# Attention's first step put in another order on all engines, and the weight sums of blocks 0 and 1 of the first expert started elsewhere

## The chip, the cores and the metric

The kernel runs on one core of one Trainium2 chip. The metric is the time of one execution in device microseconds (us). The core has five engines with a queue of their own each, which they work off in order: TensorE (PE, matrix products and transposes), VectorE (DVE), ScalarE (ACT), GpSimd (POOL) and SyncE (SP, which here only starts DMAs). They wait for each other through semaphores.

## The reference

Everything is fp32. Two batches, eight heads, 576 rows of 64 numbers; 128 random features. The result of the attention goes through a mixture of four experts and then through a layer with a cosine.

```
def phi(x):
    h = x @ omega.T - sum(x * x) / 2          # x scaled by 64 ** -0.25
    return exp(h - max(h)) / sqrt(128)
kv  = phi(k).T @ v ;  z = sum(phi(k))         # per batch and head
x   = (phi(q) @ kv) / (phi(q) @ z + 1e-6)     # 1152 tokens x 512

for e in 0..3:
    out += p[:, e] * (relu(x @ w1[e]) @ w2[e])    # p: domain_probs, normalised
h = out @ w_in ;  result = (h * cos(h)) @ w_out   # w_in, w_out given in float64
```

## The kernel before, in words

Products of full precision are made from three products of a rounded part (`...h`) and a rest (`...l`): hi x hi, hi x lo, lo x hi. ACT makes the rounded part with a copy, DVE or POOL the rest with a subtraction. So `xTh`/`xTl` are the parts of a transposed block of keys or queries, `sth`/`stl` those of a hidden activation `h`, `w1h`/`w1l` those of a weight.

Attention runs over eight pairs of heads (index `s`, a batch and two heads, 512 rows each) and one last block, the tail: the 64 rows of each batch that are left, of all heads (`kL`, `qL`). The loop over `s` (0 to 10) is a pipeline written out by hand: in step `s` it makes the key features of pair `s` (`features`: projection `pj_k` on PE, maximum `mx` and bias `nb` on DVE, exponentials `phk` on ACT), then the query features of pair `s` (`phq`), transposes pair `s+1` (`turn`), multiplies keys and values of pair `s-1` (`kv_of`), and so on. The squared norms come from POOL (`norms`, `x_k` and `x_q`) and end in a small sum on DVE (`sq`). Step 0 also makes the features of the tail's keys (`phiL`); step 1 multiplies them with the values (`kv_tail`: `kvL`).

The first expert's products are a stream of quanta (some six products each) that starts in step 6: each step calls it four times (`dense_quanta`), and after attention it runs alone. What has to be loaded or prepared is bound to a quantum's number by `start_at(e, q, ...)` in `plan`; `advance` moves each such job on by one yield per quantum. `load_a(0, p, "s")` starts a load of block `p` of `w1` at its quantum, and five quanta later makes four sums of its quarters (`rs`, the "weight sums"), which expert 0 needs for a scheme with fewer products for two thirds of its tokens (from quantum 28 on). For expert 0 sums and rest are on POOL. The loads take their buffers from a ring of three (`rawp`), and so does the job that makes the sums.

[...] The queue of each engine follows the order in which the code issues its instructions; there is no other scheduler.

The tail's transposes at the end of attention are `tx_L`; the divided result they take is `xsL`, its products are `numL`, and `pTL` are the transposed query features of the tail. `T1` to `T4` are sums of token blocks, made by DVE behind attention (`token_sums`).

Of the kernel before, what the change touches and what calls it, by code (L numbers as in the profile page):

```python
# [26 lines left out]
def performer_moe_kernel(ctx, tc, q, k, v, omega, probs, w1, w2, w_in, w_out, out):  # L27
# [4 lines left out]
    E, _, F = w1.shape  # L32
# [27 lines left out]
    late = {}  # L60

    def bank(name):
        return ps.tile([P, 512], F32, tag="ps", name=name)
# [51 lines left out]
    def split(eng, src, hi, lo):  # L115

        nc.scalar.activation(hi, src, ACTF.Copy)  # L117
        yield
        eng.tensor_tensor(out=lo, in0=src, in1=hi.bitcast(F32), op=ALU.subtract)  # L119
# [555 lines left out]
    def quantum_at(columns):  # L675
        return next(q for q in range(FROM64, sum(QE)) if columns_to(q) - columns_to(FROM64) >= columns)

    def start_at(e, q, make, *args):
        while q >= QE[e]:
            q -= QE[e]  # L680
            e += 1
        starts[e].setdefault(q, []).append(lambda: make(*args))

    def plan():
        start_at(0, 13, load_a, 0, 0, "s")
        start_at(0, 20, load_a, 0, 1, "s")
        start_at(0, 27, load_a, 0, 2)
        start_at(0, 35, load_a, 0, 3)
        for e in range(1, E + 2):
            for p, q in enumerate((51, 61) if e == 1 else (50, 60)):  # L690
                start_at(e - 1, q, load_a, e, p)
            for u, q in enumerate((0, 9, 23, 26)):
                start_at(e, q, load_v2 if e < E else load_v64, e, u)
            start_at(e, 6, load_a, e, 2)
            start_at(e, 17, load_a, e, 3)
        halves = [
            (kind, e, u, z)
            for e in (E, E + 1) for kind in "av" for u in range(NU) for z in range(2)
        ]
        at = 0  # L700
        for kind, e, u, z in halves:
            q = quantum_at(at)
            lead = quantum_at(at + LOAD64) - q
            at += A_GAP if kind == "a" else V_GAP
            start_at(0, q, lambda k=(kind, e, u), z=z, l=lead: convert64(k, z, l))
        start_at(E - 1, 58, second_x, 1)
        start_at(E - 1, 69, second_sums)
        start_at(E, 3, second_x, 0)

    plan()  # L710

    under = []
# [37 lines left out]
    with tc.tile_pool(name="at1", bufs=1) as at1, tc.tile_pool(name="at2", bufs=2) as at2:  # L750
# [5 lines left out]
        def warm(n):  # L756
            for _ in range(n):
                nc.tensor.matmul(wps[:, :P], zero, zero, start=True, stop=True)
# [64 lines left out]
        def norms(nm, t):  # L823

            x2 = at2.tile([P, 2 * R, D], F32, tag=f"x2{nm[0]}", bufs=1, name=f"x2_{nm}")
            nc.gpsimd.tensor_tensor(out=x2, in0=t, in1=t, op=ALU.mult)
            sq = at2.tile([P, 2 * R], F32, tag="sq", name=f"sq_{nm}")
            w = D
            while w > 8:
                w //= 2  # L830
                nc.gpsimd.tensor_tensor(
                    out=x2[:, :, 0:w], in0=x2[:, :, 0:w], in1=x2[:, :, w : 2 * w], op=ALU.add
                )
            yield
            nc.vector.tensor_reduce(out=sq, in_=x2[:, :, 0:w], op=ALU.add, axis=AX.X)
            yield sq

        def turn(nm, t):

            tp = bank(f"tp_{nm}")  # L840
            for i in range(R):
                nc.tensor.transpose(tp[:, i * P : (i + 1) * P], t[:, 2 * i : 2 * i + 2, :], ident)

            def split(xh=None, xl=None):
                if xh is None:
                    xh = at2.tile([P, R * P], F32R, tag="xTh", name=f"xTh_{nm}")
                    xl = at2.tile([P, R * P], F32R, tag="xTl", name=f"xTl_{nm}")
                nc.scalar.activation(xh, tp, ACTF.Copy)
                nc.vector.tensor_tensor(out=xl, in0=tp, in1=xh.bitcast(F32), op=ALU.subtract)
                return xh, xl  # L850

            return split
# [69 lines left out]
        NPR = len(pairs)  # L922
        xss, phks, phqs, kts, qts = {}, {}, {}, {}, {}
# [129 lines left out]
        def norms_ahead(nm, t):  # L1053
            sqs[nm] = norms(nm, t)
            next(sqs[nm])
# [5 lines left out]
        fk = fq = iter(())  # L1061
        turned = {}

        def turn_ahead(s):
            splits = []
            if s == 0:
                omega_pairs()
            if s < NPR and ("k", s) not in turned:
                splits.append(("k", turn(f"k{s}", kts[s])))
            if s == 0:  # L1070
                warm(1)
            splits.append(("q", turn(f"q{s}", qL if s == NPR else qts[s])))
            if s == 0:
                warm(1)
            for x, split in splits:
                if s == 0 and x == "q":
                    late["q0"] = split
                else:
                    turned[x, s] = split()

        def query_features(s):
            phqs[s] = at1.tile([P, 2 * R, M], F32, tag="phq", name=f"phq_{s}")
            steps = features(f"q{s}", turned.pop(("q", s)), phqs[s])
            next(steps)
            return steps
# [4 lines left out]
        for s in range(NPR + 3):  # L1090
            for _ in fq:
                pass
            if s < first:
                advance(wload)
            dense_quanta(s, DQ)
            kvs = kv_of(s - 1) if 1 <= s <= NPR else iter(())
            next(kvs, None)
            if s != 1:
                next(kvs, None)
            if s >= first:  # L1100
                advance(wload)
            dense_quanta(s, DQ)
            fk = iter(())
            if s < NPR:
                phks[s] = at1.tile([P, 2 * R, M], F32, tag="phk", name=f"phk_{s}")
                fk = features(f"k{s}", turned.pop(("k", s)), phks[s])
                next(fk)
            if s == 0:

                turned["kL"] = turn("kL", kL)(xkL[:, 0, :], xkL[:, 1, :])  # L1110
                turned["q", 0] = late.pop("q0")()
                norms_ahead("kL", kL)
                phiL = at1.tile([P, H, M], F32, name="phiL")
                fL = features("kL", turned.pop("kL"), phiL)
                next(fL)
            if s == 1:
                kv_tail(phiL)
                next(kvs, None)
            if s + 1 < NPR:
                norms_ahead(f"k{s + 1}", kts[s + 1])  # L1120
            if s < NPR:
                norms_ahead(f"q{s + 1}", qL if s + 1 == NPR else qts[s + 1])
            dense_quanta(s, DQ)
            next(fk, None)
            if 1 <= s <= NPR:
                turn_phi(s - 1)
            elif s == NPR + 1:
                tail_turn_phi()
            next(fk, None)
            px = iter(())  # L1130
            if 2 <= s <= NPR + 1:
                b, hp = pairs[s - 2]
                px = put_x(f"{s - 2}", hp, xss.pop(s - 2), b * R, R)
            elif s == NPR + 2:
                px = tail_put_x()
            next(px, None)
            fq = iter(())
            if s == 0:
                turned["k", 1] = turn("k1", kts[1])()
            if s <= NPR:  # L1140
                fq = query_features(s)
            for _ in px:
                pass
            dense_quanta(s, DQ)
            if s < NPR:
                turn_ahead(s + 1)
            if s == 0:
                for _ in fL:
                    pass
            if 1 <= s <= NPR:  # L1150
                nums(s - 1)
            elif s == NPR + 1:
                tail_nums()
            if s + 2 < NPR:
                load(s + 2)
            if s + 1 < NPR:
                load_v(s + 1)
            advance(wload)
            if s < 2 * NU:
                wload.append(load_a(0, s, "p") if s < NU else load_v2(0, s % NU))  # L1160
                advance(wload)
            if s == 1:
                nc.vector.tensor_reduce(out=psum_, in_=pr, op=ALU.add, axis=AX.X)
                nc.vector.tensor_scalar(out=psum_, in0=psum_, scalar1=1e-9, scalar2=None, op0=ALU.add)
                nc.vector.reciprocal(out=psum_, in_=psum_)
                nc.vector.tensor_tensor(
                    out=pn, in0=pr, in1=psum_.to_broadcast([P, NTILE, E]), op=ALU.mult
                )
# [38 lines left out]
```

## Time and profile before

| | |
|---|---|
| time, median of 3 runs | 671.59 us (670.2 to 671.76) |
| the profiled execution | 671.61 us, its span 669.8 us |
| PE busy | 660.6 us, 99% of the span |
| DVE busy | 526.2 us, 79% |
| ACT busy | 322.1 us, 48% |
| POOL busy | 183.8 us, 27% |

Attention fills the first 110 us or so of the span; with step 6, at about 60 us, the expert's products come in between. In a row of the timeline stand the start and the duration, the engine, the line, the operation, what it writes and reads, and how often it follows itself; in brackets how long the engine had idled before it, and for whom. Products are pipelined: a product's duration is longer than the distance to the next.

### The profile page before, as it was taken

What the parts mean: (1) busy time and instruction counts of PE and PEld (TensorE: products, weight loads), DVE (VectorE), ACT (ScalarE), POOL (GpSimd) and SP (SyncE); (2) the same over time, 40 slices, a digit from 0 to 9 for tenths busy, and PEclk for the clock granted to TensorE, in tenths of its full rate; (3) what the DMA queues carried; (4) which work ended last, traced back from release to release, by engine and by line L of the source; (5) the groups of instructions that cost most, each with busy time, mean ns of one, the idle gap of its engine ahead of it and who ended that gap; (6) DMA issues with size and microseconds to landing.
All of it is one profiled execution on the core that took longest, in us unless ns stands there. A gap on an engine that the chain in (4) does not pass through costs nothing.

```text
span 669.8 us, 9978 instructions
## 1 busy us (share of the span) xinstructions
PE 660.6 (99%) x3639; PEld 604.9 (90%) x3639; DVE 526.2 (79%) x965; ACT 322.1 (48%) x634; POOL 183.8 (27%) x231
## 2 busy tenths in 40 slices
PE   8999999899999999999999999999999999999998
PEld 8899998798899988899988999888999888999887
DVE  5998648879979879889899788788677793496962
ACT  5777664435433544345343354444365663355530
POOL 8778443401220111111111111100044340144420
PEclk9999999899999999999999999999999999999999
DMA  8654201231534533435525336310711000700111
GB/s 191 190 143 110 81 12 34 78 99 63 189 128 156 188 106 115 172 125 173 160 95 171 117 129 213 110 48 1 312 34 32 0 1 20 295 1 1 47 48 47
DMA packets 55441, 70.95 MB, mean 106 GB/s; under 512 B 15200, under 2 KB 40032, under 8 KB 55392
## 3 DMA queue, kind: packets, MB, share of 16 engines
q1 hardware_dynamic: 46800, 40.92, 19.8%
q0 software_dynamic: 8448, 29.37, 13.0%
q8 instruction: 28, 0.46, 0.3%
q14 instruction: 21, 0.17, 0.1%
q10 hardware_dynamic: 144, 0.03, 0.0%
HBM read 55.36 MB, written 14.94 MB: 105 GB/s over the span
## 4 chain that ended last, share of the span: by engine, by line
PE 87%; DVE 7%; POOL 2%; ACT 2%; issue 1%; DMA 0%; DVEq 0%; POOLq 0%
PE g L583 42%; PE g L431 13%; PE num L973 2%; PE g_0a L431 2%; PE g_0c L431 2%; PE g_1a L431 2%; PE kv L944 2%; PE g_3a L431 2%; PE g_1c L431 2%; PE g_3c L431 2%; PE g_2a L431 2%; PE g_2c L431 2%; PE pj_q L867 1%; PE pj_k L867 1%; PE g_0e L431 1%
## 5 line engine op out<-in xcount | busy, mean ns | idle before, releaser
L381 POOL TENSOR_TENSOR rtf64r<-rtf64r 128x384 f32<-128x384 f32 x32 | 38.4, 1199 | 117.5 <-DVE rtf64r L378 73.6
L555 ACT ACTIVATE sth<-h 128x512 fp32r<-128x512 f32 x72 | 44.8, 627 | 50.5 <-PE g L583 46.1
L556 DVE SCALAR_TENSOR_TENSOR stl<-h,sth 128x512 fp32r<-128x512 f32 x72 | 51.8, 724 | 11.3 <-ACT sth L555 9.6
L119 DVE TENSOR_TENSOR stl<-h,sth 128x512 fp32r<-128x512 f32 x36 | 35.3, 985 | 13.7 <-ACT sth L117 13.7
L583 PE MATMUL g<-v2h,stl 128*128 128x512 f32 (+1 forms) x110 | 42.9, 390 | 2.6 <-DVE stl L556 2.3
L583 PE MATMUL g<-v3h,sth 128*128 128x512 f32 (+1 forms) x110 | 43.1, 392 | 0.0
L583 PE MATMUL g<-v3l,sth 128*128 128x512 f32 (+1 forms) x110 | 42.9, 390 | 0.0
L583 PE MATMUL g<-v0h,stl 128*128 128x512 f32 (+1 forms) x110 | 42.7, 388 | 0.1
L583 PE MATMUL g<-v3h,stl 128*128 128x512 f32 (+1 forms) x110 | 42.7, 388 | 0.0
L583 PE MATMUL g<-v2h,sth 128*128 128x512 f32 (+1 forms) x110 | 42.7, 388 | 0.0
L583 PE MATMUL g<-v2l,sth 128*128 128x512 f32 (+1 forms) x110 | 42.6, 388 | 0.0
L583 PE MATMUL g<-v0h,sth 128*128 128x512 f32 (+1 forms) x110 | 42.6, 387 | 0.0
L583 PE MATMUL g<-v0l,sth 128*128 128x512 f32 (+1 forms) x110 | 42.5, 386 | 0.0
L583 PE MATMUL g<-v1h,stl 128*128 128x512 f32 (+1 forms) x110 | 42.4, 386 | 0.0
L583 PE MATMUL g<-v1h,sth 128*128 128x512 f32 (+1 forms) x110 | 42.4, 386 | 0.0
L583 PE MATMUL g<-v1l,sth 128*128 128x512 f32 (+1 forms) x110 | 42.4, 386 | 0.0
L239 ACT ACTIVATE f64t<-f64r 128x512 fp32r<-128x512 f32 x16 | 10.7, 667 | 49.2 <-DVE f64r L228 49.2
L371 ACT ACTIVATE h<-g 128x384 f32<-128x384 f32 x32 | 15.6, 489 | 35.7 <-PE g L431 35.7
L213 ACT ACTIVATE f64t<-f64r 128x512 f32<-128x512 f32 x32 | 21.3, 666 | 22.0 <-DMA f64r<-in_moe_w_in_dram 8.3
L614 DVE SCALAR_TENSOR_TENSOR acc<-g,pn,acc 128x512 f32<-128x512 f32 x27 | 20.2, 748 | 13.7 <-PE g L583 13.5
L117 ACT ACTIVATE sth<-h 128x512 fp32r<-128x512 f32 x36 | 22.4, 623 | 16.6 <-PE g L583 12.5
L431 PE MATMUL g<-xh,w0h 128*128 128x384 f32 x88 | 29.8, 338 | 0.0
(431 smaller groups left out, 2123.7 us busy)
## 6 DMA issues: line engine op xcount, KB each, us to landing
rv<-in_moe_w_dram SPq DMA_DIRECT2D x16, 512.0 KB, 3.8
f64r<-in_moe_w_in_dram POOLq DMA_DIRECT2D x16, 512.0 KB, 4.1
f64r<-in_moe_w_out_dram POOLq DMA_DIRECT2D x16, 512.0 KB, 3.8
kt<-in_k_dram SPq DMA_DIRECT2D x8, 256.0 KB, 2.9
qt<-in_q_dram SPq DMA_DIRECT2D x8, 256.0 KB, 3.3
ve<-in_v_dram SPq DMA_DIRECT2D x16, 128.0 KB, 2.8
ra_2as<-in_moe_w_dram SPq DMA_DIRECT2D x8, 256.0 KB, 3.6
ra_3as<-in_moe_w_dram SPq DMA_DIRECT2D x8, 256.0 KB, 3.9
```

What stands on the lines that cost most here:

```text
L117: nc.scalar.activation(hi, src, ACTF.Copy)
L119: eng.tensor_tensor(out=lo, in0=src, in1=hi.bitcast(F32), op=ALU.subtract)
L213: nc.scalar.activation(t.bitcast(F32), hw.bitcast(F32), ACTF.Abs)
L371: nc.scalar.activation(dst, src, ACTF.Copy)
L381: nc.gpsimd.tensor_tensor(out=vv, in0=vv, in1=kk, op=ALU.subtract)
L431: nc.tensor.matmul(dst, x[:, o], y[:, kk, :], start=start and n == 0, stop=stop and n == 3 * kn - 1, skip_group_check=reopen,)
L555: nc.scalar.activation(hi, src, ACTF.Relu)
L556: nc.vector.scalar_tensor_tensor(out=lo, in0=src, scalar=0.0, in1=hi.bitcast(F32), op0=ALU.max, op1=ALU.subtract)
L583: nc.tensor.matmul(g, x[:, p, :], y[:, o : o + w], start=n == 0, stop=n == 3 * FT - 1)
L614: nc.vector.scalar_tensor_tensor(out=acc[t], in0=src, scalar=p_, in1=acc[t], op0=ALU.mult, op1=ALU.add)
L867: nc.tensor.matmul(pj[:, i * 256 : (i + 1) * 256], a[:, cs], b_, start=z == 0, stop=z == 2)
L944: nc.tensor.matmul(kvp[:, h, :], phk[:, h * R + r, :], ve[:, h * R + r, :], start=r == 0, stop=r == R - 1)
```

## The change

Two numbers of the plan: block 0's weight sums start (load and all) at quantum 6 in place of 13, block 1's at 22 in place of 20. And in step 0 the order of the parts: the queries of pair 0 are split right after its keys; their projection comes before the tail keys'; the split of pair 1's keys comes between the two; the exponentials of pair 0's keys are now issued whole at that place, and those of its queries before the tail's.

```diff
-        start_at(0, 13, load_a, 0, 0, "s")
-        start_at(0, 20, load_a, 0, 1, "s")
+        start_at(0, 6, load_a, 0, 0, "s")
+        start_at(0, 22, load_a, 0, 1, "s")
@@ turn_ahead
-                if s == 0 and x == "q":
-                    late["q0"] = split
-                else:
-                    turned[x, s] = split()
+                turned[x, s] = split()
@@ the loop over s
                 turned["kL"] = turn("kL", kL)(xkL[:, 0, :], xkL[:, 1, :])
-                turned["q", 0] = late.pop("q0")()
+                fq = query_features(0)
                 norms_ahead("kL", kL)
+                k1 = turn("k1", kts[1])
+                for _ in fk:
+                    pass
+                turned["k", 1] = k1()
                 phiL = at1.tile([P, H, M], F32, name="phiL")
@@
-            fq = iter(())
             if s == 0:
-                turned["k", 1] = turn("k1", kts[1])()
-            if s <= NPR:
-                fq = query_features(s)
+                for _ in fq:
+                    pass
+            else:
+                fq = query_features(s) if s <= NPR else iter(())
```

DVE in step 0, before: behind pair 0's key biases (L876) stand the low parts of the tail keys and of the queries, then the tail's norm, maxima and biases, then pair 1's split, then the queries' maxima.

```order
L876 SCALAR_TENSOR_TENSOR nb_k_216<-sq_k_179,mx_k_215 128x8
L849 TENSOR_TENSOR xkL<-tp_kL,xkL 128x512
L849 TENSOR_TENSOR xTl_q_243<-tp_q_202,xTh_q_242 128x512
L835 TENSOR_REDUCE sq_kL<-x_kL 128x8
L871 TENSOR_REDUCE mx_kL<-pj_kL_256 128x4
L871 TENSOR_REDUCE mx_kL<-pj_kL_264 128x4
L876 SCALAR_TENSOR_TENSOR mx_kL<-sq_kL,mx_kL 128x8
L876 SCALAR_TENSOR_TENSOR nb_kL<-sq_kL,mx_kL 128x8
L849 TENSOR_TENSOR xTl_k_300<-tp_k_294,xTh_k_299 128x512
L835 TENSOR_REDUCE sq_q_185<-x_q_183 128x8
L871 TENSOR_REDUCE mx_q_305<-pj_q_0_307 128x4
L871 TENSOR_REDUCE mx_q_305<-pj_q_2_315 128x4
```

And now, from the same instruction on:

```order
L876 SCALAR_TENSOR_TENSOR nb_k_220<-sq_k_179,mx_k_219 128x8
L849 TENSOR_TENSOR xkL<-tp_kL,xkL 128x512
L835 TENSOR_REDUCE sq_q_185<-x_q_183 128x8
L871 TENSOR_REDUCE mx_q_248<-pj_q_0_250 128x4
L871 TENSOR_REDUCE mx_q_248<-pj_q_2_258 128x4
L876 SCALAR_TENSOR_TENSOR mx_q_248<-sq_q_185,mx_q_248 128x8
L876 SCALAR_TENSOR_TENSOR nb_q_249<-sq_q_185,mx_q_248 128x8
L849 TENSOR_TENSOR xTl_k_288<-tp_k_274,xTh_k_287 128x512
L835 TENSOR_REDUCE sq_kL<-x_kL 128x8
L871 TENSOR_REDUCE mx_kL<-pj_kL_295 128x4
L871 TENSOR_REDUCE mx_kL<-pj_kL_303 128x4
L876 SCALAR_TENSOR_TENSOR mx_kL<-sq_kL,mx_kL 128x8
```

The queries' maxima have moved ahead of the tail's, pair 1's split too, and `xTl_q` of pair 0 to a place above this piece.

POOL at the end of attention, before: the low parts of `w2`'s blocks 2 and 3, block 0's four sums and their low part (`w1l`), then block 1's.

```order
L119 TENSOR_TENSOR v2l<-rv_2_1301,v2h 128x1024
L119 TENSOR_TENSOR v3l<-rv_3_1464,v3h 128x1024
L159 TENSOR_TENSOR rs_0_1704<-ra_0s 128x256
L159 TENSOR_TENSOR rs_0_1704<-rs_0_1704,ra_0s 128x256
L159 TENSOR_TENSOR rs_0_1704<-ra_0s 128x256
L159 TENSOR_TENSOR rs_0_1704<-ra_0s,rs_0_1704 128x256
L119 TENSOR_TENSOR w1l<-rs_0_1704,w1h 128x1024
L159 TENSOR_TENSOR rs_1_1828<-ra_1s 128x256
```

And now:

```order
L119 TENSOR_TENSOR v2l<-rv_2_1301,v2h 128x1024
L159 TENSOR_TENSOR rs_0_1560<-ra_0s 128x256
L159 TENSOR_TENSOR rs_0_1560<-rs_0_1560,ra_0s 128x256
L159 TENSOR_TENSOR rs_0_1560<-ra_0s 128x256
L159 TENSOR_TENSOR rs_0_1560<-ra_0s,rs_0_1560 128x256
L119 TENSOR_TENSOR v3l<-rv_3_1467,v3h 128x1024
L119 TENSOR_TENSOR w1l<-rs_0_1560,w1h 128x1024
L159 TENSOR_TENSOR rs_1_1841<-ra_1s 128x256
```

Only block 0's sums have changed places with `v3l`. When `w1l` and what stands behind it can start is set by ACT, whose queue before held, from the evacuation of quantum 13 (`h_1134`) on:

```order
L371 ACTIVATE h_1134<-g_0_0_1_2_1585 128x384
L988 ACTIVATE pTL_1615<-tqL_1610 128x512
L917 ACTIVATE xh_110<-tx_1624 128x256
L917 ACTIVATE xh_112<-tx_1624 128x256
L371 ACTIVATE h_1134<-g_0_0_1_3_1603 128x384
L555 ACTIVATE sth<-h_1134 128x512
```

And now:

```order
L371 ACTIVATE h_1134<-g_0_0_1_2_1591 128x384
L117 ACTIVATE w1h<-rs_0_1560 128x1024
L988 ACTIVATE pTL_1622<-tqL_1617 128x512
L917 ACTIVATE xh_110<-tx_1631 128x256
L917 ACTIVATE xh_112<-tx_1631 128x256
L371 ACTIVATE h_1134<-g_0_0_1_3_1609 128x384
```

`w1h` stood ten instructions further down before, ahead of `T1h`.

## Rows read from the trace of the kernel before

**Rows 1.** The page, busy time: engine, us (share of the span) and instructions.

```profile
PE 660.6 (99%) x3639; PEld 604.9 (90%) x3639; DVE 526.2 (79%) x965; ACT 322.1 (48%) x634; POOL 183.8 (27%) x231
```

**Rows 2.** Whom PE waited for, whole run: us in total, times, longest us.

```profile
PE g L583 <- DVE stl L556: 2.3, 1, 2.3
...
PE kvL L932 <- DVE xTl_q L849: 0.8, 1, 0.8
PE pj_kL L867 <- ACT xkL L848: 0.7, 1, 0.7
```

**Rows 3.** Windows around the long wait, all engines.

```profile
core 0: us, PE busy (x) PEld busy (x) DVE busy (x) ACT busy (x) POOL busy (x), PEclk, DMA share, GB/s
...
116.00:121.08 5.08, 2.74 (x12) 1.90 (x11) 5.01 (x5) 1.15 (x2) 4.40 (x4) 1.00 0.37 103
121.08:124.78 3.70, 3.70 (x10) 2.92 (x10) 3.63 (x5) 1.11 (x2) 0.00 (x0) 0.55 0.00 0
124.78:130.00 5.22, 5.22 (x31) 5.18 (x30) 3.47 (x5) 2.75 (x4) 2.77 (x2) 0.99 0.00 0
```

**Rows 4.** Timeline of PE, 104 to 126 us: start, duration, engine, line.

```profile
107.73 0.61 PE L907 MATMUL tx_L<-ident,xsL 128*128 128x128 f32 x4
...
115.01 0.39 PE L583 MATMUL g<-v0h,sth 128*128 128x512 f32 x1
115.24 0.39 PE L583 MATMUL g<-v0l,sth 128*128 128x512 f32 x1
...
121.08 0.50 PE L583 MATMUL g<-v2h,stl 128*128 128x512 f32 x1 [2.35 <-DVE stl L556]
...
125.06 0.34 PE L431 MATMUL g_0a<-xh,w0h 128*128 128x384 f32 x1
```

**Rows 5.** Timeline of DVE, 103 to 121 us.

```profile
103.20 0.69 DVE L556 SCALAR_TENSOR_TENSOR stl<-h,sth 128x512 fp32r<-128x512 f32 x1 [0.80 <-ACT sth L555]
...
107.30 0.59 DVE L1009 TENSOR_TENSOR xsL<-numL,rdL 64x128 f32<-64x128 f32 x2
...
112.77 2.90 DVE L556 SCALAR_TENSOR_TENSOR stl<-h,sth 128x512 fp32r<-128x512 f32 x1
...
119.82 1.21 DVE L556 SCALAR_TENSOR_TENSOR stl<-h,sth 128x512 fp32r<-128x512 f32 x1
```

**Rows 6.** Timeline of POOL, 96 to 120 us.

```profile
96.21 2.40 POOL L119 TENSOR_TENSOR v3l<-rv,v3h 128x1024 fp32r<-128x1024 f32 x1 [7.41 <-ACT v3h L117]
98.55 0.75 POOL L159 TENSOR_TENSOR rs<-ra_0s 128x256 f32<-128x256 f32 x1
...
112.00 3.12 POOL L119 TENSOR_TENSOR w1l<-rs,w1h 128x1024 fp32r<-128x1024 f32 x1 [10.51 <-ACT w1h L117]
...
119.04 1.44 POOL L159 TENSOR_TENSOR rs<-ra_1s,rs 128x256 f32<-128x256 f32 x1
```

**Rows 7.** Timeline of ACT, 100 to 112 us.

```profile
100.08 0.60 ACT L988 ACTIVATE pTL<-tqL 128x512 f32<-128x512 f32 x1 [0.99 <-PE tqL L985]
...
110.88 1.05 ACT L117 ACTIVATE w1h<-rs 128x1024 fp32r<-128x1024 f32 x1
```

**Rows 8.** Timeline of DVE, steps 0 and 1.

```profile
12.13 0.22 DVE L835 TENSOR_REDUCE sq_kL<-x_kL 128x8 f32<-128x64 f32 x1 [1.77 <-POOL x_kL L831]
...
13.58 0.72 DVE L876 SCALAR_TENSOR_TENSOR mx_kL<-sq_kL,mx_kL 128x8 f32<-128x8 f32 x1
...
26.29 1.40 DVE L1164 TENSOR_SCALAR psum__170<-psum__170 128x9 f32<-128x9 f32 x1
```

**Rows 9.** Timeline of ACT, step 0.

```profile
9.21 2.18 ACT L883 ACTIVATE phk<-pj_k,nb_k 128x128 f32<-128x128 f32 x8
...
14.54 2.17 ACT L883 ACTIVATE phiL<-pj_kL,nb_kL 128x128 f32<-128x128 f32 x8 [0.34 <-DVE nb_kL L876]
```

**Rows 10.** Timeline of PE, step 1.

```profile
19.64 1.09 PE L957 MATMUL tq<-ident,phq 128*128 128x128 f32 x8
```

**Rows 11.** Timeline of POOL, step 1.

```profile
25.27 2.38 POOL L119 TENSOR_TENSOR w0l<-ra_0p,w0h 128x1024 fp32r<-128x1024 f32 x1 [0.82 <-ACT w0h L117]
```

## Prediction

> **What bounds the kernel now.** The page's busy table comes first: TensorE (PE) is busy 660.6 us of a span of 669.8 [rows 1]. So a change can only win where PE stands still, or where it runs at half clock, and only lose by making PE stand still somewhere else. The second view is who PE waited for, over the whole run [rows 2]: 2.3 us in one piece for DVE's `stl` (L556), 0.8 for `xTl_q` at the first `kvL` products, 0.7 for `xkL` at the tail keys' projection. Nothing of that size stands after 126 us: the four experts and the two cosine halves are one unbroken row of products. [...]
>
> So there are two places, and the change touches both. Early, steps 0 and 1 of attention are a chain of small dependent operations with PE idle between them. At 110 to 125 us, the last product group of expert 0's first second-layer tokens waits for its low parts. From about 20 us on PE goes from product to product, and what it saves before stays saved: everything later is issued by the same in-order queues and only slides forward.
>
> **The moved weight sums.** Why was `stl` late? DVE's two `stl` at 112.77 and 119.82 took 2.90 and 1.21 us; the same instruction took 0.69 at 103.20 [rows 5]. In both cases POOL was inside an instruction that reads SBUF: `w1l` from 112.00 to 115.12, the fourth sum of block 1 from 119.04 to 120.48 [rows 6]. Each `stl` ended 0.55 us after POOL's instruction did (115.67 against 115.12, 121.03 against 120.48). So `stl`, whose two inputs both lie in SBUF, does not run beside POOL here, it waits for it: 2.90 + 1.21 - 2 x 0.69 = 2.73 us lost on DVE in these two alone, and the three differences between them in DVE's queue are stretched too.
>
> The change takes POOL out of that stretch. By the order of the new program POOL does block 0's four sums right behind `v2l`, ahead of `v3l` (which started at 96.21 after 7.41 us of idle POOL [rows 6]), then `v3l`, then `w1l`, then block 1's sums without a pause. `w1l` waits for ACT's `w1h`, and that now stands ahead of `pTL`, where ACT idles 0.99 us for `tqL` [rows 7]; `w1h` takes 1.05, of which about 0.95 is occupancy, so it fits to within a tenth. `w1l` would then lie at about 100.1 to 102.5 and the four sums of 0.75 [rows 6] at 102.5 to 105.6, all in the old time scale. After that POOL is free until `w3l`, which is used only in block 1. The loads move with them: `ra_0s` is issued on SP ahead of `rv_3`, in the buffer of `rv_0`, and `rv_3` goes behind the release of `rv_1`. That is the release for which `ra_0s` waited before, and `rv_3` is read only just ahead of 96.21, so I cost both at nothing.
>
> The gain: with `stl` ready in time, the third token tile's 24 products run from 115.01 at the pitch of the first two, 0.23 us (115.24 - 115.01), and end at 115.01 + 24 x 0.23 = 120.53; the first product behind them started at 125.06 [rows 4]. That is 4.53 us, of which 2.35 is the wait and 10 x (0.398 - 0.23) = 1.7 the half clock (0.398 is (125.06 - 121.08)/10). Is `stl` then early enough? It ended at 121.03; without the 2.73 it ends at 118.3, and PE's wait began at 121.08 - 2.35 = 118.73. The stretched differences give more room. So what comes next on that path has about half a microsecond to spare, without counting them.
>
> The price: at 103.20 the `stl` of the first tile's second half now meets the moved sums. If it waits for the rest of one sum it loses 0 to 0.75; behind it come the tail's divisions, whose last result ends at 107.89, and PE's `tx_L` transposes are issued at 107.73 [rows 4, 5]. There is no slack there, so PE pays all of it. I take the middle, 0.35. Net: 4.2, bounds 3.8 and 4.5.
>
> [...]
>
> **Step 0.** DVE idles 1.77 us for POOL's norms of the tail keys, then works on `sq_kL` (12.13), `mx_kL`, and from 13.58 on the two bias instructions [rows 8]; ACT's `phiL` starts at 14.54 [rows 9], 2.41 after `sq_kL`. Only behind it come the first pair's query maxima, so `phq` is late, and PE reaches its transposes `tq` at 19.64 [rows 10].
>
> After the change the queries' split goes into DVE's and ACT's early idle time, pair 0's query projection takes the place on PE where the tail keys' projection waited 0.7 for `xkL` [rows 2], and the query maxima fill DVE's 1.77. What is late next is the tail: DVE must first write `xTl_k` of pair 1, which needs ACT's split behind `phk` (9.21 + 2.18 = 11.39 [rows 9], plus 0.6 for a copy of this size, as `pTL` [rows 7]): 12.0. DVE's part is another 0.65, `sq_kL` starts at 12.65, and with the same 2.41 `phiL` starts at 15.06 and ends 2.17 later [rows 9], at 17.2. That is 0.5 later than before. But now nothing of the first step stands behind it: `phq` ended about 14.2, and the `kvL` products follow `phiL` slice by slice. PE starts `tq` at about 17.4 to 17.5 in place of 19.64: 2.1 us.
>
> Does it last? The one thing that I see taking it back is L1164 in step 1, a tiny instruction that took 1.40 us because POOL's `w0l` (25.27, 2.38 us) held it up from 26.29 on [rows 8, 11]. It started 1.02 behind `w0l`. DVE will be some 2 us earlier there and POOL, I estimate, only some 1.2, since pair 1's key norms wait for the later `sq_kL`; they come to the same moment. If L1164 comes first, it takes a fraction; if `w0l` comes first, it waits 2.4, which is 1.0 more than now, and PE, which waits for pair 2's maxima behind it, keeps 1.1 of the 2.1. I take the middle, 1.6, bounds 1.0 and 2.2. The rest of step 0 is the same instructions in another order.
>
> **Sum.** 4.2 + 1.6 = 5.8 us. The profiled execution took 671.61 us, 1.81 around its span of 669.8; it equals the median shown, 671.59. 671.6 - 5.8 = 665.8 us.
>
> **Rivals.**
> - The first part gives next to nothing (0 to 0.6): if DVE and not PE sets the pace of the steps behind, what is saved at 17 us is used up there by waits for POOL. For it: L1164. Against it: the list of rows 2 names no wait of PE on DVE behind `kvL` and ahead of `stl`. Then 671.6 - 4.2 - 0.3 = 667.1.
> - The wait moves to `tx_L`. POOL's sums follow each other with gaps under a tenth; if POOL wins each of them, `stl` of 103.20 starts only when the fourth is done, at 105.6, 2.4 late. PE waits 2.4 at `tx_L`, and as after the 2.35 of 121.08 the clock falls, another 1.7. Then 4.5 - 4.1 = 0.4 is left of the second part and the time is 671.6 - 0.4 - 1.6 = 669.6. Against it: at 115.12 `stl` got in between `w1l` and the sum behind it.
> - Slower: `w1h` stands ahead of `pTL` in ACT's in-order queue, and needs all four sums of block 0, which need `ra_0s`. If the sums end after 100.08 - 0.99 = 99.1 [rows 7], PE's `numL` waits as long. They decide against the change from 99.1 + 5.8 = 104.9 on; at 107, say, it would be 671.6 + 2.1 = 673.7, with the clock's fall on top. Against it: POOL is idle from 88.8 to 96.21 [rows 6], the four sums take 3.0, and `ra_0s` gets its buffer earlier than before, not later.
> - The change does both things fully, without the two prices: 671.6 - 4.6 - 2.2 = 664.8, part of the forecast's own spread.
>
> **Chances.** Forecast, 664.2 to 667: 0.64. First part lost, 667.1: 0.18. Wait at `tx_L`, 669.6 within half a microsecond: 0.12. Slower: 0.03. Better than 664: 0.03. The range takes in the first two, the bounds of the two prices and 0.6 of spread between runs: 663.6 to 668.4. A measurement of this kernel tells 0.3% (2.0 us) from none: faster than 669.6 is 0.64 + 0.18 + 0.03 and half of the `tx_L` case, 0.91 rounded down to 0.90; same 0.07; slower 0.03.
>
> **What would show it.** PE's list of waits has no `stl` of 2 us; the granted clock is 1.00 in the windows up to 125 us; `stl` takes 0.7 twice in the third tile, and POOL's sums of block 1 lie at 101 to 106 (less the slide). PE's `tq` starts near 17.5. Wrong: a wait of over 1 us at `tx_L` or `numL`, `w1h` late on ACT, or a gap that opens in PE at 28 to 31 us behind L1164.

## The result and the profile after

The changed kernel takes 665.3 us (median of 4 runs, 665.06 to 665.62), the kernel before in the same comparison 670.89 (670.2 to 671.76): a ratio of 0.9916, 95% interval 0.9899 to 0.9934. The two profiled executions took 671.61 and 665.62 us, 5.99 apart; the prediction had said 5.8 and 665.8.

The first line below is the page's busy table of the changed kernel, beside [rows 1]: PE is busy 2.7 us less, and 1.7 of that is the half clock (granted 0.55 from 121.08 to 124.78 us, [rows 3]; now 1.00), which is gone.

```profile
PE 657.9 (99%) x3639; PEld 603.8 (91%) x3639; DVE 521.8 (79%) x965; ACT 322.3 (49%) x634; POOL 180.7 (27%) x231
```

For whom PE waited (us in total, times, longest us), to be read beside [rows 2]: `stl` of 2.3, `xTl_q` and `xkL` are gone; new is 0.8 for `pT`.

```profile
PE tp_q L842 <- DVE pT L962: 0.8, 1, 0.8
PE g L583 <- DVE stl L119: 0.3, 1, 0.3
PE kvL L932 <- ACT phiL L883: 0.2, 1, 0.2
```

The windows that answer to [rows 3]; the columns are the same. PE is busy throughout, the granted clock (the last column but two) is full, and POOL does nothing in the first of the two windows.

```profile
116.00:121.08 5.08, 5.08 (x27) 4.53 (x26) 4.96 (x6) 3.03 (x6) 0.00 (x0) 1.00 0.00 0
121.08:124.78 3.70, 3.70 (x23) 3.70 (x22) 2.41 (x5) 1.35 (x3) 2.27 (x1) 1.00 0.00 0
```

Where the time came from is read from PE's timeline: a few instructions that both programs have in the same order. Of the kernel before, beside [rows 4, 10], the products `num` of steps 1 and 2, and the first product of the third token tile that needs `stl`:

```profile
22.86 1.90 PE L973 MATMUL num<-kv,pT 128*128 128x65 f32 x16
...
31.97 2.00 PE L973 MATMUL num<-kv,pT 128*128 128x65 f32 x16
...
115.72 0.50 PE L583 MATMUL g<-v0h,stl 128*128 128x512 f32 x1
```

Of the changed kernel:

```profile
17.50 1.04 PE L957 MATMUL tq<-ident,phq 128*128 128x128 f32 x8
...
20.66 1.90 PE L973 MATMUL num<-kv,pT 128*128 128x65 f32 x16
...
29.83 0.66 PE L842 MATMUL tp_q<-ident,qt 128*128 128x128 f32 x4 [0.84 <-DVE pT L962]
30.49 2.00 PE L973 MATMUL num<-kv,pT 128*128 128x65 f32 x16
...
106.33 0.61 PE L907 MATMUL tx_L<-ident,xsL 128*128 128x128 f32 x4
...
113.61 0.39 PE L583 MATMUL g<-v0h,sth 128*128 128x512 f32 x1
...
114.07 0.39 PE L583 MATMUL g<-v0h,stl 128*128 128x512 f32 x1
...
119.05 0.33 PE L431 MATMUL g_0a<-xh,w0h 128*128 128x384 f32 x1
...
124.28 0.33 PE L431 MATMUL g_0a<-xh,w0h 128*128 128x384 f32 x1
```

Subtracted from the starts before, that is 2.14 us won at `tq`, 2.20 at the first `num`, 1.48 at the second, 1.40 at `tx_L` (107.73) and at the third token tile (115.01), and 6.01 at the first product behind it (125.06). The span is 6.0 shorter (669.8 and 663.8), so everything won by 119 us lasts to the end. Step 0 brings 2.2 and gives 0.7 back at 29 us; the moved sums bring 6.01 - 1.40 = 4.61.

On DVE, [rows 5, 8] are answered by these rows of the changed kernel: both `stl` take 0.69, and the tiny L1165 takes 2.42.

```profile
23.80 2.42 DVE L1165 TENSOR_SCALAR psum__170<-psum__170 128x9 f32<-128x9 f32 x1
...
101.80 0.69 DVE L556 SCALAR_TENSOR_TENSOR stl<-h,sth 128x512 fp32r<-128x512 f32 x1 [0.80 <-ACT sth L555]
...
115.23 0.69 DVE L556 SCALAR_TENSOR_TENSOR stl<-h,sth 128x512 fp32r<-128x512 f32 x1
```

On POOL, beside [rows 6, 11]: `w0l` starts in the same hundredth as L1165; `w1l` and block 1's sums now lie ahead of the third token tile, and one of the sums, which meets the `stl` at 101.80, takes 1.22 in place of 0.73.

```profile
23.80 2.39 POOL L119 TENSOR_TENSOR w0l<-ra_0p,w0h 128x1024 fp32r<-128x1024 f32 x1
...
98.71 2.39 POOL L119 TENSOR_TENSOR w1l<-rs,w1h 128x1024 fp32r<-128x1024 f32 x1 [1.50 <-PE tqL L985]
101.06 0.73 POOL L159 TENSOR_TENSOR rs<-ra_1s 128x256 f32<-128x256 f32 x1
101.86 1.22 POOL L159 TENSOR_TENSOR rs<-rs,ra_1s 128x256 f32<-128x256 f32 x1
```

One more thing has to be read before the experiments. The runs of the kernel before fall in two groups: of the 50 that accompanied the experiments 28 took 669.95 to 670.30 us and 22 took 671.45 to 671.80. In each run's record the mean granted clock over the whole span is 0.996 or 0.997 in all of the 22 and 1.000 in all of the 28. The profile shown ahead, at 671.61, is of the upper group; and 670.89, the median given above, lies between two runs of either group, where no run was.

### The profile page after: what moved, and what is told of

It reads as the page before. It is cut to its first block, busy times and chain, and to the rows that moved or that the text cites. A ratio compares the mean times of both kernels' runs of the same rounds, so it can differ in the third digit from the quotient of the medians.

```text
span 663.8 us, 9979 instructions
## 1 busy us (share of the span) xinstructions
PE 657.9 (99%) x3639; PEld 603.8 (91%) x3639; DVE 521.8 (79%) x965; ACT 322.3 (49%) x634; POOL 180.7 (27%) x231
## 4 chain that ended last, share of the span: by engine, by line
PE 90%; DVE 5%; POOL 2%; ACT 1%; issue 1%; DMA 0%; DVEq 0%; POOLq 0%
PE g L583 44%; PE g L431 13%; PE num L973 2%; PE g_0a L431 2%; PE g_0c L431 2%; PE g_1a L431 2%; PE kv L944 2%; PE g_3c L431 2%; PE g_3a L431 2%; PE g_2c L431 2%; PE g_2a L431 2%; PE g_1c L431 2%; PE pj_q L867 1%; PE pj_k L867 1%; PE g_0e L431 1%; PE g_0b L431 1%
## 5 line engine op out<-in xcount | busy, mean ns | idle before, releaser
L556 DVE SCALAR_TENSOR_TENSOR stl<-h,sth 128x512 fp32r<-128x512 f32 x72 | 49.0, 686 | 10.5 <-ACT sth L555 8.8
```

The source lines that it names most:

```text
L556: nc.vector.scalar_tensor_tensor(out=lo, in0=src, scalar=0.0, in1=hi.bitcast(F32), op0=ALU.max, op1=ALU.subtract)
```

## Experiments

Times are medians; each set of runs had the kernel before beside it, in both of its groups.

**Each part alone.** The first kernel has only the plan's numbers:

```diff
-        start_at(0, 13, load_a, 0, 0, "s")
-        start_at(0, 20, load_a, 0, 1, "s")
+        start_at(0, 6, load_a, 0, 0, "s")
+        start_at(0, 22, load_a, 0, 1, "s")
```

> The two numbers of the plan changed (6 and 22), step 0 in its old order. Theory (the two parts add; the sums part is worth the wait of 2.35 us at the third token tile and the half clock behind it): in the profiles the first product behind that tile moved from 125.06 to 119.05, of which 1.40 was there already at 113.61, so this kernel should gain 4.6: 667.0 us beside 671.6, no wait of PE for `stl` of 2 us, granted clock 1.00 from 116 to 125 us. Rival (the sums only fit because step 0 slid everything): a gain of 3.5 or less, 668.1 or more, with a wait of PE at `tx_L` near 107.7.

667.09 us (667.0 to 667.18). No wait for `stl`, a granted clock of 1.00 from 110 to 128 us, and the third tile runs from 115.04, without any slide from step 0, to

```profile
120.48 0.33 PE L431 MATMUL g_0a<-xh,w0h 128*128 128x384 f32 x1
```

4.58 us earlier than before. That is the theory's number, against the upper group (671.6); against the lower one the gain is 3.0. The rival falls: the sums fit without step 0.

The second kernel has the new step 0 with 13 and 20.

> Step 0 in its new order, the plan's numbers as before (13 and 20). Theory: PE's `tq` at 17.5 in place of 19.64, then 0.7 to 0.8 us given back while DVE's L1165 waits for POOL's `w0l`; 1.4 us are left from 31 us on, and the wait of 2.35 us at `stl` with its half clock stays: 670.2 us. Rival (what step 0 saves is used up by later waits for POOL): within 0.4 of before, 671.2 or more.

668.88 us, a miss by 1.3, and in three groups: five runs at 668.1 to 668.4, three at 669.4 to 669.5, two at 670.8 to 671.0. Two things were wrong in the expectation. Step 0's gain at the second `num` was 2.22 in this profile (669.36 us) and not 1.48, because `tq` began 0.30 earlier and the collision with `w0l` fell out otherwise (below):

```profile
29.75 2.00 PE L973 MATMUL num<-kv,pT 128*128 128x65 f32 x16
```

And the wait for `stl` is there, but what follows it differs from execution to execution.

The third kernel keeps step 0 and block 1's 22, and puts block 0 back to 13 (`start_at(0, 13, load_a, 0, 0, "s")`).

> New step 0; block 0's sums as before (13), block 1's at 22. Theory (what matters is that `w1l` and with it the queue behind it on POOL comes early, and that hangs on block 0's number): `w1l` stays at about 110 to 113, the sums behind it, PE waits 2 us or more for `stl`: about 670.2 us, as with step 0 alone. Rival (block 1's number carries the gain): 665.4 us.

668.37 us, in groups as with step 0 alone: `w1l` at 110.21, 3.12 long, a wait of 2.33 for `stl`. So block 1's number gives nothing by itself and block 0's is needed; whether block 0's is enough stays open, as 6 with 20 was not run. The expected 670.2 was as wrong as above, for the same two reasons. Of the eight runs above 669 us in these two sets five show a mean granted clock of 0.997 and three one of 1.000, so not all of this spread is the clock.

**Is the half clock part of the price?** Windows behind that same wait, first with step 0 alone (profiled at 669.36 us), then with block 1's number alone (668.29); PE's row of the wait ahead of each:

```profile
118.86 0.50 PE L583 MATMUL g<-v2h,stl 128*128 128x512 f32 x1 [2.33 <-DVE stl L556]
```
```profile
119.30:123.70 4.40, 4.40 (x16) 3.81 (x15) 4.29 (x6) 1.98 (x3) 0.00 (x0) 0.62 0.00 0
```
```profile
119.29 0.50 PE L583 MATMUL g<-v2h,stl 128*128 128x512 f32 x1 [2.33 <-DVE stl L556]
```
```profile
119.30:123.70 4.40, 4.40 (x22) 3.99 (x23) 4.33 (x5) 1.81 (x3) 0.00 (x0) 1.00 0.00 0
```

The same 2.33 us of idle PE, behind it 16 products at 0.62 in the one execution and 22 at 1.00 in the other. That suggested what the two groups of the kernel before are, and the next kernel tests it: before, with the gap filled.

```diff
+                                if (e, m, i, p) == (0, 2, 1, 0) and x is lo:
+                                    for _ in range(10):
+                                        nc.tensor.matmul(
+                                            g, zl, wh[:, o : o + w], start=False, stop=False
+                                        )
@@
+    zl = const.tile([P, P], F32R, name="zl")
+    nc.gpsimd.memset(zl.bitcast(F32), 0.0)
```

> The kernel before with ten products whose weights are zero (they add nothing to the sum) in front of the product that waits 2.35 us for `stl` at 118.73; 10 x 0.23 = 2.3 us of work in the gap. The kernel before gave two groups of times, 670.0 to 670.2 and 671.6 to 671.8. Theory (the upper group is the executions in which the clock falls behind this wait, because PE stood still): with the gap filled the clock stays 1.00 from 121 to 125 us and only the lower group is left, 670.0 to 670.4 in every run. Rival (the two groups have another cause): both groups again, or 671.7 with the ten products added on top.

670.15 us, ten runs of 670.04 to 670.52 (two of them 0.1 above what was expected), and none in the upper group, while of the 23 runs of the kernel before beside it 9 were; the mean granted clock is 0.999 or 1.000 in all ten. Its PE timeline and windows:

```profile
118.62 2.50 PE L585 MATMUL g<-v2h,zl 128*128 128x512 f32 x10
121.14 0.50 PE L588 MATMUL g<-v2h,stl 128*128 128x512 f32 x1
```
```profile
116.00:121.08 5.08, 5.08 (x22) 3.81 (x21) 5.01 (x5) 1.11 (x2) 4.45 (x4) 1.00 0.35 103
121.08:124.78 3.70, 3.68 (x19) 3.23 (x19) 3.63 (x6) 1.15 (x2) 0.00 (x0) 1.00 0.00 0
```

`stl` is as late as before, and the ten products cost nothing; only the clock is other. So the upper group is the executions in which the clock falls behind this wait. It costs 1.5 us (671.6 against 670.1), in nearly half of the executions.

**Is it POOL's reading?** The changed kernel with eight additions on POOL (128x256, results unused), released by ACT's `T1h` in the stretch that the change had cleared:

```diff
+        th = t_t[1][0].rearrange("p k c -> p (k c)").bitcast(F32)
+        for _ in range(8):
+            nc.gpsimd.tensor_tensor(out=scr, in0=th[:, :256], in1=th[:, 256:512], op=ALU.add)
@@
+    scr = const.tile([P, 256], F32, name="scr")
```

> The changed kernel with eight more instructions on POOL of the form of the sums (128x256, two SBUF inputs, results unused), released by ACT's `T1h` at about 112.3 us, in the stretch that the change cleared. Theory (a DVE instruction with two SBUF inputs waits for POOL's whole instruction when that reads SBUF): T1l and the two differences behind it take about 1.4 us each and `stl` of the third tile 1.2, as in the kernel before (there 1.48, 1.38, 1.37, 1.21), so `stl` ends near 117.9 in place of 115.92, PE waits about 1.1 us for it at 116.8, and more if the differences behind it are late for T2's products: 666.5 us or more without a fall of the clock, up to 668.5 with one. Rival (the gain at this place came from the moved loads or ACT's order, not from POOL's reading): 665.4 us, `stl` 0.69.

670.16 us (669.08 to 671.26). On DVE the rows are those of the kernel before again:

```profile
113.13 1.38 DVE L266 TENSOR_TENSOR rtf64r<-xh,rtf64r 128x768 f32<-128x768 f32 x1
114.54 1.38 DVE L284 TENSOR_TENSOR rtf64r<-rtf64r,xl 128x768 f32<-128x768 f32 x1
115.84 1.23 DVE L559 SCALAR_TENSOR_TENSOR stl<-h,sth 128x512 fp32r<-128x512 f32 x1
```

(0.96, 0.96 and 0.69 in the changed kernel). PE waited 0.4 us for this `stl`, not the 1.1 expected. The total is too long for another reason, my placing: the additions stood ahead of block 1's sums in POOL's queue, which so began at 123.27, and in the profile (of the longest run) PE waited 1.3 for `w3l` and 1.6 for `h` besides. The next kernel has the same fault, and its total can't be used either: in place of the additions one tiny one and 24 MEMSETs (`nc.gpsimd.memset(scr, 0.0)`).

> The same place with one tiny addition (128x8, released by `T1h`) and 24 MEMSETs of 128x256 behind it, which write SBUF and read nothing. Theory (it is the reading of two operands by both engines that excludes them): `stl` 0.69 us, no wait of PE at 116.8, 665.4 us as the changed kernel. Rival (POOL being busy at all holds DVE up): `stl` 1.2 and the time of the kernel with the eight additions.

667.74 us (666.6 to 669.63), sums at 123.14; in the profile, again of the longest run, waits of 1.1 for `w3l` and 1.4 for `h`. But the rows tell what was asked. POOL, then DVE:

```profile
114.36 8.82 POOL L295 MEMSET scr<- 128x256 f32 x24
```
```profile
115.26 0.96 DVE L284 TENSOR_TENSOR rtf64r<-rtf64r,xl 128x768 f32<-128x768 f32 x1
116.14 0.68 DVE L560 SCALAR_TENSOR_TENSOR stl<-h,sth 128x512 fp32r<-128x512 f32 x1
```

DVE doesn't notice 8.8 us of MEMSETs: L284 takes 0.96 and `stl` 0.68 beside them, 1.38 and 1.23 beside the additions. So it was POOL's additions, which read SBUF, that held up these DVE instructions with two inputs in SBUF, and not that POOL was busy: beside the MEMSETs, which only write, they lost nothing.

The additions once more, now issued behind block 1's sums (in `load_a`, behind `op(s_4, ...)`):

> The eight additions on POOL again, released by `T1h` as before, but now behind block 1's four sums in POOL's queue, so that `w3l` does not wait for them by order. Theory: the sums lie at 101 to 104.5 as in the changed kernel, `stl` of the third tile takes 1.2 us and PE waits 0.4 for it, then 1.1 for `xl` at `g_0c`, and the wait at `w3l` (1.3) and what followed it are gone: 666.8 to 667.5 us without a fall of the clock. Rival (reading on POOL matters only through its queue): 665.4 us.

667.39 us (667.18 to 668.47), within the expectation. The waits are the two expected, and none for `w3l`:

```profile
118.09 0.50 PE L587 MATMUL g<-v2h,stl 128*128 128x512 f32 x1 [0.41 <-DVE stl L560]
...
125.14 0.44 PE L435 MATMUL g_0c<-xl,w1h 128*128 128x384 f32 x1 [1.17 <-DVE xl L119]
```

The profile is of the longest run, 668.47, and in it step 0 came late: two products that the changed kernel has at 30.49 and 124.28 stand at

```profile
31.22 2.00 PE L978 MATMUL num<-kv,pT 128*128 128x65 f32 x16
...
127.18 0.33 PE L435 MATMUL g_0a<-xh,w0h 128*128 128x384 f32 x1
```

The first is 0.73 late, before any of the additions, the second 2.90. The additions thus cost 2.2 us in the row, 1.58 of it idle and the rest lost at the same two places, and 2.0 by the medians on one chip (667.39 and 665.40, below). So the additions on POOL in this stretch cost PE time by themselves, about 2 us.

**Who starts first.** One small addition (128x128) between `w1l` and block 1's first sum, so that `stl` comes while a sum is in flight:

```diff
+            if (e, p, what) == (0, 1, "s"):
+                eng.tensor_tensor(out=scr[:, :128], in0=raw[:, :128], in1=raw[:, 128:256], op=ALU.add)
             op(s1, a21, a22, ALU.add)
@@
+    scr = const.tile([P, 256], F32, name="scr")
```

> The changed kernel with one small addition on POOL (128x128, result unused) between `w1l` and the first sum of block 1, so that a sum is in flight when `stl` of the first tile's second half comes to it at 101.80; in the changed kernel `stl` started 0.06 us ahead of the second sum. [...] Rival (POOL's next sum always starts first): `stl` ends only behind the fourth sum, 2 us late, PE waits as long at `tx_L`: 667.4 us or more.

665.62 us (665.51 to 666.55). DVE, then POOL:

```profile
101.58 0.95 DVE L558 SCALAR_TENSOR_TENSOR stl<-h,sth 128x512 fp32r<-128x512 f32 x1 [0.80 <-ACT sth L557]
```
```profile
101.25 0.73 POOL L159 TENSOR_TENSOR rs<-ra_1s 128x256 f32<-128x256 f32 x1
102.06 1.06 POOL L159 TENSOR_TENSOR rs<-rs,ra_1s 128x256 f32<-128x256 f32 x1
```

`stl` waits for the sum in flight (to 101.98), ends 0.55 behind it, and the next sum waits for `stl` (1.06 in place of 0.73). The two engines take turns here; the rival, POOL winning each time, falls. The loss is 0.26 in the row (0.95 against 0.69) and about 0.2 us in time, less than the 0.35 of the prediction: 0.40 of the sum was left when `stl` started, and 0.40 + 0.55 - 0.69 = 0.26.

**Step 0's parts.** Pair 1's key transposes and split put back behind the tail's features:

```diff
-                k1 = turn("k1", kts[1])
                 for _ in fk:
                     pass
-                turned["k", 1] = k1()
@@
             if s == 0:
+                turned["k", 1] = turn("k1", kts[1])()
                 for _ in fq:
```

> The changed kernel with pair 1's key transposes and their split put back to their old place, behind the tail's features. Theory (the `xTl_k` of pair 1 is what the second projection `pj_k` on PE waits for, ahead of the tail's `kvL`): `sq_kL` and `phiL` come 0.4 us earlier, but `xTl_k` ends near 15.1 in place of 12.6, PE stands still ahead of `pj_k` and `tq` starts at about 18.8 in place of 17.5. The collision with `w0l` behind it swallows a part: 0.4 to 1.3 us slower, 665.8 to 666.7. Rival (`phiL` sets the pace, so its earlier start pays): 665.0 us.

665.86 us (665.61 to 667.13).

```profile
15.65 0.39 PE L867 MATMUL pj_k<-wsh,xTl_k 128*128 128x256 f32 x1 [1.08 <-DVE xTl_k L849]
...
18.72 1.03 PE L957 MATMUL tq<-ident,phq 128*128 128x128 f32 x8
```

In the rows it is as expected: PE waits ahead of `pj_k`, `tq` is 1.2 later, and next to nothing of that is left at the second `num` (30.57 against 30.49), since L1164 now comes later to `w0l` and takes 1.15 in place of 2.42. In the time the loss is not shown: the median is 0.5 above that of the changed kernel on the same chip (665.40, below), but the four runs overlap its five, and the longest, 667.13, has a mean granted clock of 0.997. The other parts of the new step 0 were not run one by one.

**The collision at 23.8 us.** The four gate instructions moved from step 1 to step 6:

```diff
-            if s == 1:
+            if s == 6:
                 nc.vector.tensor_reduce(out=psum_, in_=pr, op=ALU.add, axis=AX.X)
```

> The changed kernel with the four gate instructions (L1164 to L1167) in step 6 in place of step 1, behind everything that step issues on DVE. Theory (DVE's L1165, 2.42 us because POOL is inside `w0l`, is what opens PE's gap of 0.84 us at `tp_q`, 29.8 us): the gap goes, `num` of the third step starts 0.8 to 1.0 us earlier than 30.49, and it stays so: 664.4 to 664.6 us beside 665.4. Rival (DVE is the pace there anyway, or the next STT beside POOL takes the wait over): same time within 0.3 us, a gap of the same size at `tp_q` or at the `tq` of that step.

664.09 us (663.88 to 665.19), 0.3 below what was expected. PE has no wait over 0.4 left behind its start. To exclude chance and the chip, both once more on one chip:

> The changed kernel once more, on the same chip as the one with the late gates. 665.1 to 665.6 us in every run, since it has no wait of PE behind which the clock could fall.

> The kernel with the gate instructions in step 6 once more. 664.1 us, 1.0 to 1.3 below the changed kernel on the same chip, if the gain of the first time was that of the gap at `tp_q`; the same 665.3 if it was chance.

The changed kernel 665.40 us (665.08 to 666.35; one of five runs above what was expected, at a mean granted clock of 1.000), with the late gates 663.86 (663.62 to 664.19): 1.5 us less where 1.0 to 1.3 was expected, and no overlap. Against the kernel before, 670.3 in these runs, it is 0.9898 (0.9884 to 0.9911). This version beats both. The changed kernel's second profile, at 665.08 us, shows the collision with another outcome; DVE, POOL and PE:

```profile
23.65 0.17 DVE L1165 TENSOR_SCALAR psum__170<-psum__170 128x9 f32<-128x9 f32 x1
23.86 0.22 DVE L1166 RECIPROCAL psum__170<-psum__170 128x9 f32<-128x9 f32 x1
24.11 2.01 DVE L1167 TENSOR_TENSOR pn<-pr,psum__170 128x36 f32<-128x36 f32 x1
```
```profile
23.68 2.38 POOL L119 TENSOR_TENSOR w0l<-ra_0p,w0h 128x1024 fp32r<-128x1024 f32 x1
```
```profile
29.92 2.00 PE L973 MATMUL num<-kv,pT 128*128 128x65 f32 x16
```

L1165 starts 0.03 us ahead of `w0l` and gets through in 0.17; then L1167, with two inputs, waits instead (2.01, against 0.20 in the profile after). This is the common outcome: seven of the eight profiles with the whole new step 0 and the gates in step 1 show it, and the one with L1165 at 2.42 is the profile after. The second `num` is 2.05 earlier than before, not 1.48; 0.15 of that is an earlier `tq` (17.35). With the late gates and nearly the same start (`tq` at 17.30) it begins at

```profile
29.06 1.90 PE L973 MATMUL num<-kv,pT 128*128 128x65 f32 x16
```

That is 0.86 earlier, about what the gap at `tp_q` was thought to be worth. More comes one step later: the third `num`, first of the changed kernel and then with the late gates, is 1.21 earlier. So DVE's delay cost PE more than the gap that the list of waits shows.

```profile
38.87 1.98 PE L973 MATMUL num<-kv,pT 128*128 128x65 f32 x16
```
```profile
37.66 1.90 PE L973 MATMUL num<-kv,pT 128*128 128x65 f32 x16
```

## Why the prediction was right, step by step

- **Which waits count.** Right for the change: PE's two early waits and the one for `stl` are gone, and what was won by 31 us and at the third tile stayed won to the end. But "what it saves before stays saved", from about 20 us on, is too early: 0.7 was given back at 29 us. And the waits of rows 2 were not all there was to win: with the gates out of DVE's way another 1.5 us came, of which that list shows nothing. (No run has the late gates with the old step 0.)
- **Moved sums, 4.2 (3.8 to 4.5).** 4.61 in the profile and 4.58 with the plan's numbers alone, just above the upper bound. The cause was as given: the additions bring the slow `stl` back (1.23) and cost about 2 us, the MEMSETs leave it fast (0.68). (The additions do not repeat the whole loss: they began behind the `stl` that took 2.90.) The 4.53 of the working is right, but the two terms named in it, 2.35 and 1.7, make only 4.05. The rest lay at the wait too and ahead of it: the `stl` that ended at 115.67 already held PE up, by 0.25 at 115.72 (114.07 + 1.40 = 115.47). POOL's places were right too: `w1l` forecast at 100.1 less the slide of 1.4, found at 98.71; block 1's sums 102.5 less 1.4, found at 101.06. The term that was mis-sized is the price of 0.35 at the first tile's `stl`: it was 0, as `stl` started at 101.80, 0.06 ahead of the second sum, and it was the sum that waited (1.22). With the additions behind the sums the second sum waited alike (1.23), but nothing in the working foresaw it; it is luck, and the slightly later sum of the experiment shows the other outcome, 0.2 to 0.3.
- **The half clock, 1.7 of the 4.5.** Real in the profiled execution (granted 0.55), but not a property of the kernel: in 28 of the 50 runs the mean granted clock is 1.000. Counted from the lower group of the kernel before the sums are worth 3.0 (670.1 to 667.09), and the whole change 4.8 (670.1 to 665.3). The prediction started from an execution of the upper group and said nothing of the other, although one of the three times shown, 670.2, belonged to it. The time forecast, 665.8, does not suffer from it, since the loss was in the 671.6 that it was taken from; the gain forecast, 5.8, holds against the upper group alone.
- **Step 0, 2.1 won and 1.6 kept (1.0 to 2.2).** `tq` forecast at 17.4 to 17.5, found at 17.50. That L1164 (now L1165) and `w0l` would meet was foreseen, with 2.4 of waiting if `w0l` is first; it took 2.42, and 1.48 were kept at the second `num`, where the working had 1.1: DVE's loss of 1.0 more than before reached PE with 0.66 only. PE waited there for `pT`, which stands behind pair 2's maxima in DVE's queue, and not for the maxima. From `tq` to the second `num` it is 12.33 us before, 12.99 in the profile after and 12.55 to 12.57 in the seven profiles in which L1165 is first. So the collision gives back 0.66 or 0.23, and what else differs is where `tq` begins. The working let L1165 through at a fraction of the price and did not see that L1167 then waits 2.0. That the middle, 1.6, is near the 1.48 is in part luck: the profile after had the rarer of the two outcomes.
- **The rivals.** The wait at `tx_L` did not come: `tx_L` kept its 1.40. `w1h` fitted ahead of `pTL`: `pTL` starts 0.63 behind `tqL` in both profiles (100.08 and 99.45; 98.68 and 98.05). Step 0's gain was not used up: the second kernel above kept about 1.9 of it in its lowest group (670.1 to 668.2).

## What to carry to other kernels

Where a small DVE instruction with inputs in SBUF takes several times its usual duration (here `stl` 2.90 in place of 0.69, L1165 2.42 in place of 0.17), look at what POOL reads in the same moment, and try POOL's instruction in a stretch where DVE works from PSUM (here `xsL`, 0.59 us beside the sums as before without them) or idles; its order in the queue against other POOL work has to be checked at the same time. A wait of a busy PE can have a second price in the clock, which not every execution pays (here, behind 2.35 us, 1.5 us in 22 of 50 runs): compare several runs before taking it from one profile. And where instructions of DVE and POOL that held each other up start within a few hundredths of a microsecond (here L1165 and `w0l`, 0.00 and 0.03 apart), give both outcomes a number, or move one of them out of the way, which here was worth another 1.5 us.

## What the runs showed that was not expected

- The same idle time of PE (2.33 us) was followed by a granted clock of 0.62 in one execution and of 1.00 in the other; ten products without any use in the gap kept it at 1.00 in the profile, and all runs in one group.
- RECIPROCAL (one input in SBUF) ran in 0.22 us at 23.86 while POOL was inside `w0l` (23.68 to 26.06, second profile of the changed kernel); TENSOR_SCALAR, also with one, took 2.42 beside `w0l` in the profile after and 0.17 where it started first. So in these profiles not only instructions with two inputs waited.
- Step 0 doesn't run alike in each execution: `tq` began at 17.50 and 17.35 us in the two profiles of the changed kernel, at 17.73 and 17.30 in the two with the late gates, and between 17.20 and 18.84 in all profiles with the new order. The cause was not looked for; it is part of the spread of the times at a mean granted clock of 1.000 (665.08 to 666.35 us in the five runs of the changed kernel beside the late gates).
